# A GraphSAGE layer: destination one-hots in steps of 36 buckets, made apart from the source one-hots, and narrow tiles for the leftover one-hots

## Chip, cores, metric

The kernel runs on one core of a Trainium2 chip. The time is device microseconds of one launch. Comparisons are made between runs on the same chip; the profile is that of one further execution.

## What is computed

800,000 edges over 12,500 nodes with 64 features each. Each edge adds the features of its source node to its destination node; the sums are scaled by `deg_inv` and go through one 64 x 64 matrix, each node's own features through another.

```python
def reference(x, src, dst, deg_inv, w_self, w_neigh):
    N = x.shape[0]
    nsum = _segment_sum(x[src], dst, N)
    h_neigh = nsum * deg_inv[:, None]
    return x @ w_self + h_neigh @ w_neigh
```

`src` and `dst` are random, so nothing is known of the order of the edges.

## The kernel before

**Sorting.** Up to about 800 us the edges are sorted: each is a key made of its destination block (2 x 82 nodes, 77 blocks), its source block (128 nodes, 98 blocks) and the places in both. Edges with the same two blocks form a *bucket*; there are 77 x 98 = 7546 buckets (`NBID`), ordered by destination block. A bucket is held as 128 slots, 64 for each half (82 nodes) of its destination block. VectorE does the sorting and merging (L260, L316, L328). The buckets come in three parts, of 29, 20 and 10 buckets a row (`KPRS`), starting at buckets 0, 3712 and 6272 (`BASE`). Only the first part is ready when the last stage begins; the other two are merged and decoded beside it.

**Decoding.** `decode_buckets` (L766) writes the source places of a part to a DRAM tensor `sl` (one row of 128 slots a bucket) and turns its destination places by TensorE, so that each bucket becomes one column of an SBUF tile `dlT`. This tile has `TURN` columns; bucket b lies in column b modulo `TURN`, so the last part takes the place of the first. Before, `TURN` is 6272, the first multiple of 28 from `BASE[2]` on, and `SPARE`, the distance between the two, is 0. `turn` (L799) copies up to four buckets of each row at a time; for the last part, rows that lie before the wrap or across it get copies of their own (L815), the others one wide copy (L808).

**The last stage**, `nodes` (L943), runs in tiles of 8 buckets, some 950 tiles, each with these steps:

- `one_hots` (L924) makes, for 28 buckets at once, the source one-hots `ohs` (L935, one VectorE operation on the slots of `sl`, spread over all partitions by four DMAs of SP's queue into `slb`, L933) and right behind it the destination one-hots `ohd` (L940, one VectorE operation that compares columns of `dlT` with 0 to 81). `slb` and `ohs` have three buffers, `ohd` four.
- `gather` (L956) multiplies each bucket's source one-hot with the features of its source block on TensorE (L966), which fetches the source features of 128 edges into PSUM (`ct`, three buffers). ScalarE copies eight buckets of it to SBUF (`xg`, L976). After the last part is decoded (`self.changed`), VectorE takes some of these copies (L974): every other of those tiles at which the next tile will need new source one-hots.
- `sums` (L1027), two to five tiles later, multiplies the fetched features with the destination one-hots (L1047), 64 slots for each half, and adds them up in PSUM over six destination blocks (`OCT`). Then the matrix, the degree and the output follow (`finish`).

One-hots are made ahead: `gather` calls for more when fewer than `cnt + AHEAD` buckets are ready (8 + 44, and 8 + 36 once `self.changed`).

**Leftovers.** Edges that do not fit into their bucket's slots are collected apart. `pick` (L989) gathers their features by an indirect DMA of GpSimd's queue (L997), `spread` (L1002) makes their destination one-hots `ohl` (L1006) for only those destination blocks of the octet that the group can touch, from block f up to block e, and `add` (L1011) multiplies them into the same sums (L1015). The tile `ohl` has room for all six blocks of the octet in both halves, with five buffers (`HELD`).

**Order.** All of this stands under a schedule written by hand: each engine's instructions run in the order in which the program issues them. Between two tiles the program also issues merging operations on VectorE (L316, L328), as many as a pace allows (`PACE`, less what other VectorE work was put down in `self.spent`); the one-hots are not part of that count.

Of the kernel before, what the change touches and what calls it, by code (L numbers as in the profile page):

```python
# [14 lines left out]
FH = mybir.dt.float16  # L15
I32 = mybir.dt.int32
U32 = mybir.dt.uint32
OP = mybir.AluOpType
# [7 lines left out]
HN = 82  # L26
NDB = -(-N // (2 * HN))
NBID = NDB * NB
# [5 lines left out]
NP = len(KPRS)  # L34
ROWS = (128,) * NP
BASE = [128 * sum(KPRS[:p]) for p in range(NP)]
TURN = -(-BASE[2] // 28) * 28
SPARE = TURN - BASE[2]
assert 128 * KPRS[2] < BASE[1]
NCOL = 128 * sum(KPRS)  # L40
# [30 lines left out]
BEHIND = 5e3  # L71
NEARLY = 24
LAG = 4
HELD = 5
OCT = 6
OCTM = 256 // OCT + 1
# [297 lines left out]
class Kernel:  # L374
# [371 lines left out]
    def find_and_gather(self, part, vp):  # L746
# [7 lines left out]
        junk = vp.tile([128, max(n for _, n in WIN.w2[part])], BF, name="junk")  # L754
        for k in range(kpr + LAG):
            if k == 1:
                self.store_rows(part, nc.gpsimd)
            if k < kpr:
                self.count_below(part, k, acc, junk)
            if k >= LAG:  # L760
                g = k - LAG
                nc.scalar.activation(ix[:, g:g + 1], acc[:, g:g + 1], AF.Relu, bias=self.c2[part][:, 3, g:g + 1])
# [158 lines left out]
        self.left[part] = (place, s)  # L921
        yield 1

    def one_hots(self, pool):  # L924


        nc = self.nc
        for c in range(0, NBID, 28):
            n = min(28, NBID - c)
            b = pool.tile([128, 28 * 128], BF, name="slb", bufs=3)[:, :n * 128]  # L930
            src = self.sl[c:c + n]
            for j in range(4):
                nc.sync.dma_start(b[j::4], bass.AP(tensor=src.tensor, offset=src.offset, ap=[[0, 32], [1, n * 128]]))  # L933
            s = pool.tile([128, 28, 128], FH, name="ohs", bufs=3)[:, :n]
            nc.vector.tensor_scalar(s.rearrange("p c s -> p (c s)"), b, self.pidx[:, :1], None, op0=OP.is_equal)  # L935
            d = pool.tile([128, 14, HN, 2], FH, name="ohd", bufs=4)[:, :n // 2]
            at = c % TURN
            wide = [128, n // 2, HN, 2]
            ix = self.dlT[:, at:at + n].rearrange("p (c t) -> p c t", t=2)[:, :, None, :].to_broadcast(wide)
            nc.vector.tensor_tensor(d, self.iota[:, None].to_broadcast(wide), ix, op=OP.is_equal)  # L940
            yield [(s[:, j], d[:, j // 2, :, j % 2]) for j in range(n)]

    def nodes(self, pool, aps, mps):  # L943


        nc = self.nc
        source = self.one_hots(pool)
        ready = []
        pend = []
        late = []  # L950
        done = []
        acc = None
# [3 lines left out]
        def gather(b0, cnt, vector):  # L956

            nonlocal turn
            ct = aps.tile([128, 1024], F32, name="ct", bufs=3)
            ahead = AHEAD - 8 * vector  # L960
            while len(ready) < min(cnt + ahead, NBID - b0):
                ready.extend(next(source))
            cols = ready[:cnt]
            del ready[:cnt]
            for i in reversed(range(cnt)):
                nc.tensor.matmul(ct[:, i * 128:(i + 1) * 128], cols[i][0],  # L966
                                 self.xh[:, (b0 + i) % NB].rearrange("p a f -> p (a f)"), start=True, stop=True)
            xg = pool.tile([128, 1024], FH, name="xg", bufs=6)
            if vector and (len(ready) < min(8 + ahead, NBID - b0 - cnt) or NBID - b0 < 56):
                turn += 1  # L970
            else:
                vector = False
            if vector and turn % 2:
                nc.vector.tensor_copy(xg[:, :cnt * 128], ct[:, :cnt * 128])  # L974
            else:
                nc.scalar.activation(xg[:, :cnt * 128], ct[:, :cnt * 128], AF.Copy)  # L976
            return b0, xg, [d for _, d in cols]

        uses = []
        for o in range(-(-NDB // OCT)):  # L980
            lo, hi = o * OCT * NB, min((o + 1) * OCT * NB, NBID)
            for p in range(NP):
                for c in range(CHK[p]):
                    f = max(BASE[p] + c * GRP[p] * KPRS[p], lo)
                    e = min(BASE[p] + min((c + 1) * GRP[p], 128) * KPRS[p], hi)
# [3 lines left out]
        def pick(b0):  # L989
            if self.picked == len(done) or len([u for u in uses if u[5]]) >= HELD:  # L990
                return
            u = next((u for u in uses if not u[5]), None)
            if u and u[1] in self.left and b0 + LEAD >= u[4] * NB:
                _, p, c = u[:3]
                x = u[5] = pool.tile([128, 128], FH, name="lx", bufs=HELD)
                u[6] = len(done)
                nc.gpsimd.indirect_dma_start(  # L997
                    out=x, out_offset=None, in_=self.xt,
                    in_offset=bass.IndirectOffsetOnAxis(ap=self.left[p][1][:, c:c + 1].bitcast(U32), axis=0))
                self.picked = len(done)  # L1000

        def spread(u):  # L1002
            o, p, c, f, e = u[:5]
            u[7] = pool.tile([128, 2, OCT * HN], FH, name="ohl", bufs=HELD)
            n = slice((f - o * OCT) * HN, (e - o * OCT) * HN)
            nc.vector.tensor_scalar(u[7][:, :, n], self.wide.rearrange("p (h n) -> p h n", h=2)[:, :, n],  # L1006
                                    self.left[p][0][:, c:c + 1], -float(o * (OCT * HN + 4096)),
                                    op0=OP.subtract, op1=OP.is_equal)
            self.spent += 300

        def add(u, stop=False):  # L1011
            o, _, _, f, e = u[:5]
            n = slice((f - o * OCT) * HN, (e - o * OCT) * HN)
            for h in range(2):
                nc.tensor.matmul(acc[h][:, n], u[5], u[7][:, h, n], start=False, stop=stop)  # L1015

        def extras(b0, cnt):
            o = b0 // (OCT * NB)
            for u in uses[:HELD]:
                if u[5] and not u[7] and len(done) >= u[6] + 10 and b0 + 80 >= (u[4] - 1) * NB:  # L1020
                    spread(u)
                    break
            if uses and uses[0][7] and uses[0][0] == o and b0 + cnt > (uses[0][4] - 1) * NB and (
                    len(uses) > 1 and uses[1][0] == o):
                add(uses.pop(0))

        def sums(job):  # L1027
# [10 lines left out]
            if b0 + 24 >= end:  # L1038
                for u in uses:
                    if u[0] == o and not u[7]:  # L1040
                        assert u[5] and len(done) >= u[6] + 4
                        spread(u)
# [25 lines left out]
        for t, (b0, cnt) in enumerate(tiles):  # L1068
            pend.append(gather(b0, cnt, self.changed))
            if (len(pend) > 5) if self.changed else t % 2:  # L1070
                while len(pend) > (3 if self.changed else 2):
                    b0 = pend[0][0]
# [5 lines left out]
            b0 = tiles[t][0]  # L1078
# [130 lines left out]
    def after_sort(self, es, mps, aps):  # L1209
# [7 lines left out]
        with tc.manual_schedule():  # L1217
# [28 lines left out]
            for _ in self.merge_runs(LENA[0], u0, w0, NSUP):  # L1246
                if rows and not self.hold and next(rows, None) is None:
# [3 lines left out]
                    dl = es.enter_context(tc.tile_pool(name="dl", bufs=1, side="right"))  # L1251
                    self.dlT = dl.tile([128, TURN], BF, name="dlT")
            assert not rows
# [159 lines left out]
```

## Time and profile before

| | us |
|---|---|
| median of 3 runs | 1865.99 |
| lowest, highest | 1864.18, 1870.74 |
| the profiled execution | 1856.37 |
| its span, first to last instruction | 1854.6 |

In the profile, PE is TensorE's matmuls and PEld its weight loads, DVE is VectorE, ACT ScalarE, POOL GpSimd, SP the engine that issues most loads. A row of a group has the line, the engine, the operation, output and inputs, the shapes and the count, then busy time and the mean length in ns, then the idle time ahead of it and what ended it. A row of a wait names who waited for whom, with the total in us, how often, and the longest. A row of a stretch has the busy time and count of each engine, the granted TensorE clock as a share, the share of the DMA engines and GB/s.

### The profile page before, as it was taken

How to read it: one execution, taken by the hardware profiler on the slowest of the kernel's cores; microseconds unless marked ns; L12 is line 12 of the kernel's file. 1: busy time of each engine (PE TensorE's matmuls, PEld its weight loads, DVE VectorE, ACT ScalarE, POOL GpSimd, SP SyncE). 2: the span in 40 equal slices, each digit the busy share in tenths (PEclk: the TensorE clock that was granted, in tenths of full speed). 3: DMA queues.
4: the chain of work that ended last, by engine and by line, in shares of the span. 5: the costliest groups of instructions: out<-in, count | busy, mean ns of one | idle time of the engine just before them, and what ended most of it. 6: DMA issues, size and time to landing. Idle time of an engine off the chain costs nothing.

```text
span 1854.6 us, 54153 instructions
## 1 busy us (share of the span) xinstructions
PE 986.6 (53%) x23413; PEld 851.9 (46%) x23413; DVE 1718.2 (93%) x1718; ACT 1116.7 (60%) x1587; POOL 576.2 (31%) x447
## 2 busy tenths in 40 slices
PE   3046000000000000058979979897898899888996
PEld 1015000000000000057868868776887788777885
DVE  6999999999999999989989999998898799978885
ACT  5263000113001005458979989899999899977885
POOL 2000000055502005404456535473332523532331
PEclk7567555555555555579989999999999999999998
DMA  5207100021002002169978888996889788977894
GB/s 174 54 0 169 39 0 0 38 79 51 18 4 73 10 0 82 47 216 266 274 249 253 251 248 254 296 282 227 264 250 284 234 265 242 326 200 257 274 268 118
DMA packets 176789, 307.79 MB, mean 166 GB/s; under 512 B 127885, under 2 KB 133596, under 8 KB 175772
## 3 DMA queue, kind: packets, MB, share of 16 engines
q1 hardware_dynamic: 98268, 275.58, 44.9%
q0 software_dynamic: 78272, 28.65, 9.6%
q8 instruction: 185, 3.03, 0.7%
q14 instruction: 64, 0.52, 0.1%
HBM read 277.01 MB, written 26.52 MB: 164 GB/s over the span
## 4 chain that ended last, share of the span: by engine, by line
DVE 19%; PE 13%; DMA 11%; issue 10%; SPq 5%; POOL 4%; ACT 4%; DVEq 0%; POOLq 0%; ACTq 0%
DMA slb<-sl 10%; PE ct L966 7%; DVE u L328 7%; PE acc L1047 5%; SPq L933 5%; DVE ohs L935 4%; DVE ohd L940 3%; ACT xg L976 2%; DVE u L362 2%; POOL u L565 1%; POOL lx L997 1%; POOL out L1123 1%; DVE u L316 1%; DMA sl<-l 1%; PE acc L1015 1%
## 5 line engine op out<-in xcount | busy, mean ns | idle before, releaser
L976 ACT ACTIVATE xg<-ct 128x1024 f16<-128x1024 f32 x919 | 862.6, 1074 | 104.4 <-PE ct L966 80.0
L966 PE MATMUL ct<-xh,ohs 128*128 128x128 f16 x7546 | 532.6, 224 | 87.9 <-DVE ohs L935 23.7
L966 PEld LDWEIGHTS <-ohs 128*128 128x128 f16 x7546 | 451.8, 100 | 125.4 <-issue 52.5
L328 DVE TENSOR_TENSOR u<-u 128x1512 f32<-128x1512 f32 (+57 forms) x316 | 425.7, 1362 | 12.9 <-ACT u L312 8.6
L1047 PE MATMUL acc<-ohd,xg 64*128 64x82 f16 x15092 | 395.2, 201 | 47.7 <-ACT xg L976 20.4
L1047 PEld LDWEIGHTS <-xg 64*128 64x128 f16 x15092 | 324.6, 96 | 104.6 <-issue 29.2
L997 POOL DMA_INDIRECT lx<-xt,ls x127 | 232.0, 1826 | 425.6 <-PE acc L1015 352.5
L940 DVE TENSOR_TENSOR ohd<-iota,dlT 128x2296 f16<-128x2296 bf16 x270 | 362.2, 1341 | 0.0
L935 DVE TENSOR_SCALAR ohs<-slb,pidx 128x3584 f16<-128x3584 bf16 x270 | 321.8, 1192 | 40.2 <-DMA slb<-sl 19.0
L509 PE MATMUL stp<-cx,swapa 128*128 128x16 f32 (+1 forms) x12 | 3.1, 335 | 398.0 <-DVE swapa L505 398.0
L260 DVE TENSOR_TENSOR a<-b 128x1040 f32<-128x1040 f32 (+41 forms) x130 | 194.7, 1539 | 3.5 <-DVE b L260 0.5
L260 DVE TENSOR_TENSOR b<-a 128x1040 f32<-128x1040 f32 (+46 forms) x150 | 194.6, 1345 | 3.2 <-ACT a L262 0.4
L538 POOL DMA_INDIRECT u<-d,ixa x48 | 72.5, 1511 | 390.8 <-ACT junka L526 335.4
L509 PEld LDWEIGHTS stp<-cx,swapa 128*128 128x128 f32 x12 | 2.6, 271 | 398.5 <-DVE swapa L505 398.5
L312 ACT ACTIVATE u<-u 128x256 f32<-128x256 f32 (+14 forms) x60 | 33.0, 618 | 170.6 <-DVE u L316 134.8
L1123 POOL DMA_DIRECT2D out<-o x27 | 99.1, 3800 | 103.1 <-ACT o L1117 89.8
L802 PE MATMUL tr<-idb,l 128*128 128x128 bf16 x59 | 7.6, 263 | 188.9 <-ACT l L796 188.9
L262 ACT ACTIVATE b<-a 128x2 f32<-128x2 f32 (+31 forms) x41 | 15.9, 402 | 127.1 <-DVE a L260 120.4
L802 PEld LDWEIGHTS <-l 128*128 128x128 bf16 x59 | 4.3, 114 | 191.2 <-ACT l L796 190.8
L316 DVE TENSOR_TENSOR u<-u 128x2016 f32<-128x2016 f32 (+11 forms) x40 | 61.9, 1563 | 16.2 <-DMA u<-da,ixb 8.8
L262 ACT ACTIVATE a<-b 128x1 f32<-128x1 f32 (+24 forms) x34 | 8.6, 259 | 105.4 <-DVE b L260 99.9
L565 POOL DMA_INDIRECT u<-da,ixb x24 | 36.9, 1539 | 88.6 <-ACT ixb L513 85.0
(158 smaller groups left out, 839.4 us busy)
## 6 DMA issues: line engine op xcount, KB each, us to landing
slb<-sl SPq DMA_DIRECT2D x1076, 224.0 KB
xt<-xh SPq DMA_DIRECT2D x1, 3136.0 KB
out<-o POOLq DMA_DIRECT2D x25, 123.0 KB
own<-os SPq DMA_DIRECT2D x12, 256.0 KB
out<-os SPq DMA_DIRECT2D x12, 256.0 KB
rd<-dst SPq DMA_DIRECT2D x5, 512.0 KB
rs<-src SPq DMA_DIRECT2D x5, 512.0 KB
lx<-xt,ls POOLq DMA_INDIRECT x127
```

The costliest lines, as they stand in the source:

```text
L260: nc.vector.tensor_tensor(view(dst, lo + sh, [[st, g], [1, l]]), x, y, op=op)
L316: nc.vector.tensor_tensor(at(oth, to, n), x, y, op=op)
L328: nc.vector.tensor_tensor(to, at(cur, ln + lo, n), at(cur, lo + k, n), op=op)
L538: nc.gpsimd.indirect_dma_start(out=u[:, i * w:(i + 1) * w], out_offset=None, in_=src, in_offset=bass.IndirectOffsetOnAxis(ap=self.start[pa ...
L933: nc.sync.dma_start(b[j::4], bass.AP(tensor=src.tensor, offset=src.offset, ap=[[0, 32], [1, n * 128]]))
L935: nc.vector.tensor_scalar(s.rearrange("p c s -> p (c s)"), b, self.pidx[:, :1], None, op0=OP.is_equal)
L940: nc.vector.tensor_tensor(d, self.iota[:, None].to_broadcast(wide), ix, op=OP.is_equal)
L966: nc.tensor.matmul(ct[:, i * 128:(i + 1) * 128], cols[i][0], self.xh[:, (b0 + i) % NB].rearrange("p a f -> p (a f)"), start=True, stop=True)
L976: nc.scalar.activation(xg[:, :cnt * 128], ct[:, :cnt * 128], AF.Copy)
L997: nc.gpsimd.indirect_dma_start(out=x, out_offset=None, in_=self.xt, in_offset=bass.IndirectOffsetOnAxis(ap=self.left[p][1][:, c:c + 1].bit ...
L1047: nc.tensor.matmul(acc[h][:, db % OCT * HN:(db % OCT + 1) * HN], xg[r, i * 128:(i + 1) * 128], d[r], start=db % OCT == 0 and sb == 0, stop ...
L1123: nc.gpsimd.dma_start(out, o[:n, at], accum_op=OP.add)
```

## The change

Three things. The constant 28 in `TURN` becomes 36, which makes `TURN` 6300 and `SPARE` 28. `one_hots` falls into two generators: `source_hots` keeps its steps of 28, `dest_hots` makes destination one-hots in steps of 36 (`DCH`). `gather` draws from both, from whichever has fewer buckets ready, until both have enough. And the tile `ohl` becomes two blocks wide, filled from its start.

```diff
-TURN = -(-BASE[2] // 28) * 28
+TURN = -(-BASE[2] // 36) * 36
...
+DCH = 36
...
-    def one_hots(self, pool):
+    def source_hots(self, pool):
...
-            s = pool.tile([128, 28, 128], FH, name="ohs", bufs=3)[:, :n]
-            nc.vector.tensor_scalar(s.rearrange("p c s -> p (c s)"), b, self.pidx[:, :1], None, op0=OP.is_equal)
-            d = pool.tile([128, 14, HN, 2], FH, name="ohd", bufs=4)[:, :n // 2]
+            s = pool.tile([128, 28 * 128], FH, name="ohs", bufs=3)[:, :n * 128]
+            nc.vector.tensor_scalar(s, b, self.pidx[:, :1], None, op0=OP.is_equal)
+            yield [s[:, j * 128:(j + 1) * 128] for j in range(n)]
+
+    def dest_hots(self, pool):
+        nc = self.nc
+        for c in range(0, NBID, DCH):
+            n = min(DCH, NBID - c)
+            d = pool.tile([128, DCH // 2, HN, 2], FH, name="ohd", bufs=4)[:, :n // 2]
             at = c % TURN
             wide = [128, n // 2, HN, 2]
             ix = self.dlT[:, at:at + n].rearrange("p (c t) -> p c t", t=2)[:, :, None, :].to_broadcast(wide)
             nc.vector.tensor_tensor(d, self.iota[:, None].to_broadcast(wide), ix, op=OP.is_equal)
-            yield [(s[:, j], d[:, j // 2, :, j % 2]) for j in range(n)]
+            yield [d[:, j // 2, :, j % 2] for j in range(n)]
...
-        source = self.one_hots(pool)
-        ready = []
+        sources, dests = self.source_hots(pool), self.dest_hots(pool)
+        ready, spare = [], []
...
-            while len(ready) < min(cnt + ahead, NBID - b0):
-                ready.extend(next(source))
-            cols = ready[:cnt]
+            need = min(cnt + ahead, NBID - b0)
+            while min(len(ready), len(spare)) < need:
+                if len(ready) <= len(spare):
+                    ready.extend(next(sources))
+                else:
+                    spare.extend(next(dests))
+            cols = list(zip(ready[:cnt], spare[:cnt]))
             del ready[:cnt]
+            del spare[:cnt]
...
-            u[7] = pool.tile([128, 2, OCT * HN], FH, name="ohl", bufs=HELD)
+            assert e - f <= 2
+            u[7] = pool.tile([128, 2, 2 * HN], FH, name="ohl", bufs=HELD)
             n = slice((f - o * OCT) * HN, (e - o * OCT) * HN)
-            nc.vector.tensor_scalar(u[7][:, :, n], self.wide.rearrange("p (h n) -> p h n", h=2)[:, :, n],
+            nc.vector.tensor_scalar(u[7][:, :, :(e - f) * HN], self.wide.rearrange("p (h n) -> p h n", h=2)[:, :, n],
...
-                nc.tensor.matmul(acc[h][:, n], u[5], u[7][:, h, n], start=False, stop=stop)
+                nc.tensor.matmul(acc[h][:, n], u[5], u[7][:, h, :(e - f) * HN], start=False, stop=stop)
```

## The prediction

> **What bounds the kernel now.** I read the page's busy line and its slices first, then the stretches of the last stage, then what VectorE waits for there.
>
> ```profile
> span 1854.6 us, 54153 instructions
> PE 986.6 (53%) x23413; PEld 851.9 (46%) x23413; DVE 1718.2 (93%) x1718; ACT 1116.7 (60%) x1587; POOL 576.2 (31%) x447
> ...
> PE   3046000000000000058979979897898899888996
> ...
> DVE  6999999999999999989989999998898799978885
> ACT  5263000113001005458979989899999899977885
> ```
>
> TensorE has no work before about the seventeenth slice (some 800 us) except at the very start: until there VectorE sorts, alone. The changed lines run only from there on. So the table that counts is that of the last stage, cut where `nodes` starts to give VectorE some of the PSUM copies.
>
> ```profile
> core 0: us, PE busy (x) PEld busy (x) DVE busy (x) ACT busy (x) POOL busy (x), PEclk, DMA share, GB/s
> 800.00:1640.00 840.00, 734.61 (x18474) 648.69 (x18476) 783.15 (x936) 771.45 (x997) 366.67 (x212) 0.96 0.86 261
> 1640.00:1840.00 200.00, 176.00 (x4667) 158.87 (x4660) 173.99 (x210) 157.35 (x185) 51.25 (x26) 0.97 0.80 244
> ```
>
> Up to 1640 us VectorE is busy for 93% of the time, ScalarE for 92%, TensorE for 87%, and the DMA engines for 86%: four resources stand within a few per cent of each other, VectorE first. After 1640 us VectorE and TensorE stand at 87 to 88%. Finer stretches of 40 us show where VectorE alone is the bound:
>
> ```profile
> 880.00:920.00 40.00, 36.49 (x897) 32.36 (x890) 38.54 (x39) 39.86 (x66) 21.22 (x11) 0.94 0.90 268
> ...
> 1040.00:1080.00 40.00, 36.21 (x942) 32.24 (x942) 40.00 (x36) 37.96 (x50) 25.04 (x8) 1.00 0.81 236
> ...
> 1240.00:1280.00 40.00, 28.83 (x706) 24.23 (x705) 32.50 (x44) 38.00 (x56) 17.52 (x13) 1.00 0.79 251
> ...
> 1560.00:1600.00 40.00, 35.98 (x958) 31.21 (x955) 39.04 (x51) 38.57 (x52) 19.44 (x14) 1.00 0.92 298
> 1600.00:1640.00 40.00, 33.80 (x826) 29.77 (x822) 33.15 (x49) 38.89 (x60) 20.91 (x17) 0.96 0.80 253
> ```
>
> Of the 26 stretches from 800 to 1840 us, 13 have VectorE busy for 38.5 us or more (the first is 880 to 920, the last 1560 to 1600). There a nanosecond less on VectorE is a nanosecond less of time. In the other 13 it waits:
>
> ```profile
> DVE xg L974 <- PE ct L966: 19.4, 14, 3.2
> DVE ohs L935 <- DMA slb<-sl: 19.0, 15, 6.2
> DVE ohs L935 <- PE ct L966: 18.9, 18, 2.9
> DVE u L316 <- DMA u<-da,ixb: 7.3, 1, 7.3
> DVE u L316 <- DMA lx<-xt,ls: 7.0, 1, 7.0
> ```
>
> Each row has the total, the number of waits and the longest. Some are TensorE being late, some loads being late; no row says that a destination one-hot (`ohd`, L940) waits for its buffer.
>
> **What the change does to the work.** Destination one-hots: 7546 buckets were 269 operations of 28 and one of 14, 270 in all; in steps of 36 they are 209 and one of 22, 210 in all. The elements stay the same, so only what an instruction costs beside its elements goes, 60 times.
>
> ```profile
> L940 DVE TENSOR_TENSOR ohd<-iota,dlT 128x2296 f16<-128x2296 bf16 x269 | 361.4, 1344 | 0.0
> L935 DVE TENSOR_SCALAR ohs<-slb,pidx 128x3584 f16<-128x3584 bf16 x269 | 321.2, 1194 | 40.2 <-DMA slb<-sl 19.0 <-PE ct L966 18.9 <-PE acc L1047 1.0
> ```
>
> The rows above have the count, then busy time and mean ns of one, then idle time ahead; the next has the shortest, median and longest of all 270.
>
> ```profile
> L940 DVE TENSOR_TENSOR ohd<-iota,dlT x270: 751/1344/1403, 804.5 to 1832.6; 128x2296 f16<-128x2296 bf16 x135
> ```
>
> The odd one of 14 buckets has half the elements (14 x 82 = 1148) and is the minimum, 751 ns. So an element costs (1344 - 751) / 1148 = 0.517 ns, and the fixed part of a row is 1344 - 2296 x 0.517 = 158 ns. Rows of neighbours overlap, though:
>
> ```profile
> 1155.76 1.35 DVE L940 TENSOR_TENSOR ohd<-iota,dlT 128x2296 f16<-128x2296 bf16 x1
> 1157.03 0.26 DVE L1006 TENSOR_SCALAR ohl<-wide,lp 128x164 f16<-128x164 f16 x1
> 1157.96 1.68 DVE L935 TENSOR_SCALAR ohs<-slb,pidx 128x3584 f16<-128x3584 bf16 x1 [0.68 <-DMA slb<-sl]
> 1159.56 1.33 DVE L940 TENSOR_TENSOR ohd<-iota,dlT 128x2296 f16<-128x2296 bf16 x1
> 1160.82 2.90 DVE L328 TENSOR_TENSOR u<-u 128x1205 f32<-128x1205 f32 x2
> ```
>
> The first number is the start, the second the length. The instruction behind an `ohd` starts 1.26 to 1.27 us after it, while its row is 1.34 us long: some 79 ns lie under the next one. VectorE therefore pays 1.265 - 2296 x 0.517 / 1000 = 0.079 us of fixed cost for each. An operation of 36 buckets (2952 elements) should have a row of 1344 + 656 x 0.517 = 1683 ns and take 1.604 us to the next start. **Saved on VectorE: 60 x 0.079 = 4.7 us** (ends: 0 if 36 buckets cost more an element than 28, and 60 x 0.158 = 9.5 us if the whole fixed part counts).
>
> How much reaches the end: half of the stretches have VectorE full, which gives 2.35 us of the 4.7 in full. In the other half something else is late about as often as VectorE; I take half, 1.2 us. Together **3.5 us**; if all is on the path 4.7, if the other limits close up at once 0.
>
> Moved: in `nodes` a source operation is made when fewer than `cnt + AHEAD` columns are ready, a destination one when fewer than that are spare. Each stream alone follows the old rule, so every L935 and each of its four loads (L933, SP's queue) is issued at the same tile as before; only the L940s move. They no longer stand right behind an L935 but at tiles of their own, up to 44 buckets ahead of the matmul that gathers and more ahead of L1047 that reads them. No wait is added: four buffers of 36 hold 144 buckets instead of 112, and the 0.0 in the L940 row says that even 112 kept nothing waiting. So the larger buffers gain nothing either, and I cost them at 0.
>
> Leftover one-hots: the operation was already cut to its one or two blocks, only the tile was wide.
>
> ```profile
> L1006 DVE TENSOR_SCALAR ohl<-wide,lp 128x164 f16<-128x164 f16 x67 | 21.2, 320 | 0.0
> L1006 DVE TENSOR_SCALAR ohl<-wide,lp 128x328 f16<-128x328 f16 x60 | 19.0, 318 | 0.0
> ```
>
> 164 and 328 are 2 halves of 82 and of 164 columns, so the instructions stay as they are: 0 us. What it gives is room (5 x 2 x 2 x (492 - 164) = 6560 bytes a partition), which the wider `ohd` takes (4 x 8 x 82 x 2 = 5248).
>
> `TURN` becomes 6300, a multiple of 36, so 28 buckets of the last part lie before the wrap. In `turn` that takes three rows out of the wide copy and makes 9 small copies (L815) of 3, with their rows here:
>
> ```profile
> L815 ACT ACTIVATE dlT<-tr x3: 188/190/205, 1612.6 to 1625.0; 128x4 bf16<-128x4 bf16 x2, 128x2 bf16<-128x2 bf16 x1
> L805 ACT ACTIVATE dlT<-tr x13: 607/776/807, 740.9 to 1280.7; 128x512 bf16<-128x512 bf16 x12, 128x128 bf16<-128x128 bf16 x1
> ```
>
> Six more of 0.19 us are 1.1 us of ScalarE around 1612 to 1625 us, where it is the bound (38.89 of 40 in the row above); behind them wait the `xg` copies. Between 0 and 1.1 I take 0.5. Operations that straddle two parts now begin at buckets 3708 and 6264. The first is due at tile (3708 - 44) / 8 = 458, the second at 777.
>
> ```profile
> core 0: us, PE busy (x) PEld busy (x) DVE busy (x) ACT busy (x), PEclk, DMA share, GB/s
> 800.00:1280.00 480.00, 180.04 (x6712) 145.69 (x6712) 0.00 (x0) 397.79 (x424) 0.95 0.87 263
> 1280.00:1640.00 360.00, 141.48 (x5316) 115.29 (x5318) 2.12 (x2) 312.84 (x336) 0.96 0.84 259
> ```
>
> These are the copies `xg`, one a tile: 424 by 1280 us, about 760 by 1640, at 1.07 us a tile in the second stretch. So those tiles run near 1316 and 1658 us, over 30 us after the last writes of `dlT` that they need (1281 and 1625 us): no new wait.
>
> **Sum.** 3.5 - 0.5 = 3.0 us less. The profiled execution took 1856.37 us (span 1854.6), so **1853.4 us** for it. The median of the runs shown is 1865.99 us, 1.0052 times as much; on that scale the forecast is **1863.0 us**, 0.16% less.
>
> **Rivals.**
>
> *The whole row counts.* The fixed 158 ns would be paid in full, 9.5 us less, 1846.9 us (1856.4 on the median's scale). For it: VectorE has stretches of 40.00 in 40. Against it: the overlapping starts above. [...]
>
> *Moved operations fill waits.* L935 waits 33 times for slb or TensorE, 37.9 us without the L940 behind it being able to start. With the streams apart, an L940 can stand ahead of a waiting L935 and use the gap. A tile is 8 of 36 buckets, so about a quarter of the waits have one directly ahead: 0.25 x (37.9 - 6.2 for the first load) = 8 us, with the 3.0 above 11 us less, 1845.4 us (1855.0). Against it: where VectorE waits it is not the bound, and the filled time is soon lost to the engine that was late.
>
> *Slower: an L940 ahead of a PSUM copy on VectorE.* After 1640 us every other tile at which the ready columns are low gives its copy to VectorE.
>
> ```profile
> L974 DVE CAST xg<-ct 128x1024 f16<-128x1024 f32 x30 | 36.5, 1221 | 17.4 <-PE ct L966 16.2 <-ACT xg L976 1.1
> ```
>
> These tiles were chosen so that the pair of one-hots comes just after the copy. An L940 with a rhythm of its own falls on such a tile in 8 of 36 cases, and the copy starts up to 1.6 us later: 30 x 8 / 36 x 1.6 = 10.7 us if TensorE, with three `ct` buffers, stops for all of it (now its matmuls wait little for those copies:
>
> ```profile
> PE ct L966 <- DVE xg L974: 4.1, 4, 1.5
> ```
>
> in these 200 us). Less the 3.0 that is 7.7 us more, 1864.1 us (1873.7). It decides only if the delay exceeds the 0.58 us that a copy waits for its matmuls on average anyway (17.4 / 30), and if ScalarE has no slack to catch up; it has 21% there, which speaks against.
>
> *It doesn't pay.* Operations of 36 cost as much for a bucket as those of 28, or TensorE and the loads close up: 0, 1856.4 us (1866.0). DMA at 0.86 and ScalarE at 92% speak for it.
>
> **How the numbers follow.** A measurement here can tell about 0.3% (5.6 us) from no change. Chances: forecast 0.48 (own range 1860 to 1866), no pay 0.17, filled waits 0.13, whole row 0.10, slower 0.12. Both fast rivals lie beyond 0.3%, and 0.04 of the forecast's tail: faster 0.27. Slower 0.12. Same 0.61. The range takes in both fast rivals at the low end (1855.0, less 1 for the bounds of their terms) and at the high end no pay with all small copies and part of the slower case, 1871: 1854 to 1871, which leaves out some 0.15.
>
> **What would show it.** L940 should count 210 with rows near 1683 ns and a sum near 353 us; the start behind it 1.60 us later. If the rows are longer than 1.75 us, the saving is gone. VectorE's busy sum between 800 us and the end should fall by about 9 us in rows (of which half is overlap), its waits stay near their present sums. If the waits of L935 fall by several us, the waits were filled; if those of TensorE on L974 (4.1 us now) rise by several, the slower rival holds. L815 should count 9. L935 and L933 should keep 270 and 1080 rows. The time before 797 us should not move: a difference there would be none of this change's, and would make the prediction wrong for a reason not treated here.

## The result, and the profile after

| | runs | median us | lowest, highest |
|---|---|---|---|
| before | 7 | 1866.93 | 1863.31, 1870.74 |
| after | 7 | 1875.92 | 1868.78, 1880.45 |

The ratio is 1.0051, with a 95% interval of 1.0032 to 1.0070: **slower by half a per cent, 9 us**, where 0.16% less was forecast, and beyond the range. The profiled execution of the changed kernel took 1868.78 us (span 1867.1), 12.4 us more than that of the kernel before. Of the runs further below, three that took over 1.5% longer than the fastest of their kernel are left out of every comparison: two of the kernel before (2115 and 2778 us) and one of `e_early` (1892 us).

The page of the changed kernel gives the span, the busy sums (engine, us, share of the span, instructions) and, of its groups, the ones that the change touches. Behind the change the lines are shifted: L936 makes the source one-hots, L949 the destination ones, L980 fetches, L990 and L988 copy, L1062 adds up, L1011 gathers the leftovers.

```profile
span 1867.1 us, 54098 instructions
...
PE 1005.2 (54%) x23413; PEld 861.5 (46%) x23413; DVE 1716.4 (92%) x1658; ACT 1117.5 (60%) x1593; POOL 606.8 (33%) x447
...
L1011 POOL DMA_INDIRECT lx<-xt,ls x127 | 268.9, 2117 | 423.9 <-PE acc L1030 346.8
...
L936 DVE TENSOR_SCALAR ohs<-slb,pidx 128x3584 f16<-128x3584 bf16 x270 | 321.1, 1191 | 56.6 <-DMA slb<-sl 21.3
L949 DVE TENSOR_TENSOR ohd<-iota,dlT 128x2952 f16<-128x2952 bf16 x210 | 353.6, 1684 | 0.0
```

VectorE has the 60 instructions less that were counted, 1658 for 1718, but its busy time fell by 1.8 us alone. Two other things moved. GpSimd (POOL) is busy 30.6 us longer with the same 447 instructions, and its leftover gather takes 2117 ns on the mean where it took 1826, as the row of the kernel before has it:

```profile
L997 POOL DMA_INDIRECT lx<-xt,ls x127 | 232.0, 1826 | 425.6 <-PE acc L1015 352.5
```

And source one-hots wait 56.6 us, where they waited 40.2; 10.4 of them are one wait at 1449 to 1459 us.

Where is the time lost? The count of fetch matmuls in a stretch (`ct`, 28 for each source one-hot) is a clock of progress. Here are the stretches for that one line, first of the kernel before, then of the changed one; the columns are TensorE's matmuls and weight loads, the granted clock, the DMA engines' share, GB/s.

```profile
800.00:1240.00 440.00, 224.59 (x3149) 189.28 (x3150) 0.95 0.88 264
1240.00:1300.00 60.00, 27.81 (x392) 23.61 (x393) 0.97 0.75 242
```

```profile
800.00:1240.00 440.00, 224.92 (x3148) 188.99 (x3148) 0.95 0.87 264
1240.00:1300.00 60.00, 26.27 (x354) 22.28 (x355) 0.94 0.70 215
```

Up to 1240 us the two kernels are level, 3149 and 3148 matmuls after 440 us. In the next 60 us the changed one does 38 fewer; at 60 us for 392 that is 5.8 us. The rest of the 12.4 us is lost in later stretches. At 1240 to 1300 us part 1 is decoded beside the last stage, and the waits there (who waited for whom: total us, times, longest) name the place. Changed kernel, 1240 to 1290 us:

```profile
PE acc L1062 <- ACT xg L990: 10.3, 4, 5.8
DVE w L783 <- ACT l L793: 6.6, 1, 6.6
...
ACT l L797 <- DMA sl<-l: 4.3, 1, 4.3
```

And the kernel before, the same stretch:

```profile
PE acc L1047 <- ACT xg L976: 8.0, 5, 2.4
...
DVE w L782 <- ACT l L792: 3.8, 2, 2.3
...
ACT l L791 <- DMA sl<-l: 1.0, 1, 1.0
```

Read from the bottom up. ScalarE waits for the store of source slots to `sl`, 4.3 us and not 1.0; TensorE then waits up to 5.8 us for ScalarE's copies `xg`, and VectorE 6.6 us for ScalarE. ScalarE's timeline in the changed kernel (start, length, operation, idle time ahead in brackets) shows that wait between the two copies of the second group of slots. In parts 1 and 2 `l16` has two buffers, and one still belongs to the store of the first group.

```profile
1253.51 0.63 ACT L793 ACTIVATE l<-w 128x512 bf16<-128x512 int32 x1
...
1259.53 0.63 ACT L793 ACTIVATE l<-w 128x512 bf16<-128x512 int32 x1
1264.51 0.63 ACT L797 ACTIVATE l<-v 128x512 bf16<-128x512 int32 x1 [4.35 <-DMA sl<-l]
1265.05 2.83 ACT L990 ACTIVATE xg<-ct 128x1024 f16<-128x1024 f32 x3
```

The first group was copied by 1254.14 (1253.51 + 0.63). Its store is issued by GpSimd, whose timeline follows, changed kernel first:

```profile
1235.34 1.58 POOL L743 DMA_INDIRECT v<-d,ix  x1 [0.30 <-ACT xg L990]
1237.22 4.05 POOL L1011 DMA_INDIRECT lx<-xt,ls  x1 [0.30 <-issue]
1241.58 3.21 POOL L1011 DMA_INDIRECT lx<-xt,ls  x1 [0.30 <-PE ct L980]
1245.09 1.44 POOL L743 DMA_INDIRECT v<-d,ix  x1 [0.30 <-ACT xg L990]
...
1255.60 1.24 POOL L1011 DMA_INDIRECT lx<-xt,ls  x1 [0.30 <-issue]
1256.78 0.66 POOL L795 DMA_DIRECT2D sl<-l  x1
```

```profile
1234.75 0.95 POOL L997 DMA_INDIRECT lx<-xt,ls  x1 [0.30 <-issue]
1236.01 1.58 POOL L997 DMA_INDIRECT lx<-xt,ls  x1 [0.30 <-issue]
...
1249.78 1.70 POOL L997 DMA_INDIRECT lx<-xt,ls  x1 [0.30 <-issue]
1252.60 0.58 POOL L794 DMA_DIRECT2D sl<-l  x1 [1.12 <-ACT l L792]
```

Before, GpSimd was idle for 1.12 us and issued the store 0.3 us behind the copy. Now it comes straight from other work, 2.6 us late (1256.78 - 1254.14). In this time its queue holds the same instructions in the same order, yet it reached the first leftover gather 2.5 us later than before (1237.22 for 1234.75), was through with the second 7.2 us later (1244.79 for 1237.59), and made up some of that in the gathers behind. These two gathers, 0.95 and 1.58 us long before, took 4.05 and 3.21. What kept them? VectorE's timeline of the changed kernel, over the same time:

```profile
1235.66 1.15 DVE L936 TENSOR_SCALAR ohs<-slb,pidx 128x3584 f16<-128x3584 bf16 x1
1236.72 0.94 DVE L329 TENSOR_TENSOR u<-u 128x756 f32<-128x756 f32 x1
1237.57 1.69 DVE L949 TENSOR_TENSOR ohd<-iota,dlT 128x2952 f16<-128x2952 bf16 x1
1239.18 0.91 DVE L329 TENSOR_TENSOR u<-u 128x728 f32<-128x728 f32 x1
1240.01 1.15 DVE L936 TENSOR_SCALAR ohs<-slb,pidx 128x3584 f16<-128x3584 bf16 x1
1241.07 0.93 DVE L329 TENSOR_TENSOR u<-u 128x744 f32<-128x744 f32 x1
1241.91 1.69 DVE L949 TENSOR_TENSOR ohd<-iota,dlT 128x2952 f16<-128x2952 bf16 x1
1243.52 1.15 DVE L936 TENSOR_SCALAR ohs<-slb,pidx 128x3584 f16<-128x3584 bf16 x1
```

The first gather ends at 1241.27, the second source one-hot L936 at 1241.16; the second gather ends at 1244.79, the third L936 at 1244.67. Both end 0.11 to 0.12 us after a source one-hot has ended. Each held GpSimd from just behind one source one-hot to the end of the next. Three operations lie between the first two L936 here, two between the next. Over the 75 source one-hots from 960 to 1240 us, the distance from start to start has a standard deviation of 0.97 us in the changed kernel and 0.67 in the one before. That this unevenness is what stretches the gathers is not shown, and `e_half28` below speaks against it.

This is no chance of two rows. In 16 profiles of this case, 522 of GpSimd's gather issues after 800 us took over 2.4 us. Of them 440 ended between 0.05 and 0.20 us after the end of a source one-hot (25 of 29 in the kernel before, 38 of 44 in the changed one), and none that close behind a destination one-hot. Of 932 issues of at most 1.3 us 98 did. Those during which VectorE was idle (187) took 0.95 us in the median. In the rows above one issue stood for 4.05 us beside four operations and ended only behind the source one-hot; which of the four held it, they do not tell, and by what means is not shown.

One thing adds to the loss. The stretches of 1260 to 1274 us in the changed kernel (busy time and count of each engine, granted clock, DMA share, GB/s):

```profile
1260.00:1262.00 2.00, 0.35 (x16) 0.20 (x12) 1.94 (x5) 0.16 (x1) 1.24 (x2) 1.00 1.08 370
1262.00:1264.00 2.00, 0.00 (x0) 0.00 (x0) 2.00 (x3) 0.00 (x0) 0.60 (x1) 1.00 0.97 336
1264.00:1266.00 2.00, 0.00 (x0) 0.00 (x0) 0.26 (x1) 1.49 (x3) 0.00 (x0) 0.77 0.92 283
1266.00:1268.00 2.00, 1.89 (x29) 1.77 (x30) 0.00 (x0) 2.00 (x4) 0.64 (x1) 0.50 0.73 266
1268.00:1270.00 2.00, 2.00 (x38) 1.80 (x37) 0.00 (x0) 1.97 (x4) 0.34 (x1) 0.50 0.17 31
1270.00:1272.00 2.00, 2.00 (x30) 1.85 (x24) 1.14 (x3) 1.97 (x5) 0.58 (x1) 0.52 0.05 8
1272.00:1274.00 2.00, 1.79 (x47) 1.43 (x45) 1.86 (x3) 2.00 (x4) 0.00 (x0) 1.00 0.18 66
```

TensorE stands still for 5.8 us, from 1260.35 to 1266.11, and when it goes on the granted clock is 0.50 until about 1272 us.

The late issue is only half of the store's delay. The store lands in 16 parts, each counted in the trace. Before, the last part came 5.3 us after the issue (1257.89); now it comes after 7.6 us (1264.36), 1.9 us behind the fifteenth. So it lands 10.2 us behind ScalarE's copy and not 5.6, and of these 4.6 us the issue makes 2.3. The DMA engines are full in this time (1.08, 0.97), but so they were before (1.03, 0.92, 0.97 and 1.03 from 1252 to 1260 us), so that does not explain it. Over the profiles below in which GpSimd issues the store, it landed 4.0 to 5.8 us after an issue in time, and 6.8 to 13.9 us after one that GpSimd's own work had made late. Why the last part comes late is open.

### The profile page after: what moved, and what is told of

Its sections match the earlier page's. It is cut to its first block, busy times and chain, and to the rows that moved or that the text cites. A ratio compares the mean times of both kernels' runs of the same rounds, so it can differ in the third digit from the quotient of the medians.

```text
span 1867.1 us, 54098 instructions
## 1 busy us (share of the span) xinstructions
PE 1005.2 (54%) x23413; PEld 861.5 (46%) x23413; DVE 1716.4 (92%) x1658; ACT 1117.5 (60%) x1593; POOL 606.8 (33%) x447
## 4 chain that ended last, share of the span: by engine, by line
PE 16%; DVE 16%; DMA 10%; issue 9%; ACT 9%; SPq 5%; POOL 2%; DVEq 0%; another core or an unknown queue 0%; ACTq 0%; POOLq 0%
DMA slb<-sl 9%; PE ct L980 9%; PE acc L1062 6%; ACT xg L990 6%; DVE u L329 6%; SPq L934 5%; DVE ohs L936 3%; DVE ohd L949 2%; DVE u L363 2%; DVE u L317 1%; ACT u L313 1%; POOL u L566 1%; PE acc L1030 1%; PE po L1129 1%; DVE ohl L1021 1%
## 5 line engine op out<-in xcount | busy, mean ns | idle before, releaser
L990 ACT ACTIVATE xg<-ct 128x1024 f16<-128x1024 f32 x919 | 863.7, 1070 | 120.1 <-PE ct L980 72.0
L980 PE MATMUL ct<-xh,ohs 128*128 128x128 f16 x7546 | 535.0, 224 | 79.9 <-ACT xg L990 22.1
L980 PEld LDWEIGHTS <-ohs 128*128 128x128 f16 x7546 | 452.7, 100 | 117.5 <-issue 47.3
L1062 PE MATMUL acc<-ohd,xg 64*128 64x82 f16 x15092 | 405.3, 201 | 61.2 <-issue 30.5
L1011 POOL DMA_INDIRECT lx<-xt,ls x127 | 268.9, 2117 | 423.9 <-PE acc L1030 346.8
L1062 PEld LDWEIGHTS <-xg 64*128 64x128 f16 x15092 | 328.1, 96 | 125.1 <-issue 52.2
L936 DVE TENSOR_SCALAR ohs<-slb,pidx 128x3584 f16<-128x3584 bf16 x270 | 321.1, 1191 | 56.6 <-DMA slb<-sl 21.3
L949 DVE TENSOR_TENSOR ohd<-iota,dlT 128x2952 f16<-128x2952 bf16 x210 | 353.6, 1684 | 0.0
L566 POOL DMA_INDIRECT u<-da,ixb x24 | 34.1, 1419 | 89.3 <-ACT ixb L514 85.4
```

Of the source, the lines that this page charges most:

```text
L936: nc.vector.tensor_scalar(s, b, self.pidx[:, :1], None, op0=OP.is_equal)
L980: nc.tensor.matmul(ct[:, i * 128:(i + 1) * 128], cols[i][0], self.xh[:, (b0 + i) % NB].rearrange("p a f -> p (a f)"), start=True, stop=True)
L1011: nc.gpsimd.indirect_dma_start(out=x, out_offset=None, in_=self.xt, in_offset=bass.IndirectOffsetOnAxis(ap=self.left[p][1][:, c:c + 1].bit ...
L1062: nc.tensor.matmul(acc[h][:, db % OCT * HN:(db % OCT + 1) * HN], xg[r, i * 128:(i + 1) * 128], d[r], start=db % OCT == 0 and sb == 0, stop ...
```

## Experiments

**Theory A**, which grew out of the first runs: the loss is made where part 1 is decoded, by the chain above: uneven source one-hots, stretched gathers, a late store, ScalarE's wait for a buffer, TensorE behind it. Its links are tested one by one, and not all of them held. **Theory B**: the new rhythm costs a little in many places. Ratios are to the kernel before, run on the same chip between them; below 1 is faster.

To compare the profiles, the text gives two numbers of each: how late GpSimd issued the first store of part 1 after ScalarE's copy, and how long the nine source one-hots around the decode took (from the start of the 118th to that of the 127th). Before they are 0.3 and 41.7 us, after 2.6 and 46.4.

### The parts of the change

**Old lengths, old order, narrow `ohl`.**

```diff
-DCH = 36
+DCH = 28
```

> The changed kernel with destination steps of 28 again: the streams draw in step, so every L940 stands right behind its source one-hots as before, while TURN 6300, the small copies in turn and the narrow ohl tile stay. If the order or the length of the destination operations makes the loss: ratio 1.000 (0.998 to 1.002). If the rest of the change makes it (copies, addresses, room): 1.005.

Measured: 0.9986 (0.9964 to 1.0008). Late 0.3, nine one-hots 42.1 us. The narrow leftover tiles and the wrap at 6300 cost nothing.

**28 in an even rhythm of their own**: the first operation makes 14 buckets.

```diff
-TURN = -(-BASE[2] // 36) * 36
+TURN = 14 + -(-BASE[2] // 28) * 28
-DCH = 36
+DCH = 28
...
-        for c in range(0, NBID, DCH):
-            n = min(DCH, NBID - c)
+        for c in (0, *range(14, NBID, DCH)):
+            n = min(DCH if c else 14, NBID - c)
```

> Destination steps of 28, but the first one of 14, so that each destination operation comes half a step away from the source operations; 271 operations of the old length, evenly spaced (TURN 6286). If it is enough that the two stand apart: 1.005. If it is the uneven spacing that 36 against 28 makes, or the length of 36: 1.000.

Measured: 0.9989 (0.9968 to 1.0010). Late 0.3, 41.8 us. Two streams half a step apart are no loss when both have the same step. But the leftover gathers are stretched here too, 2098 ns on the mean, as in the changed kernel (2117), although the source one-hots come as evenly as before (standard deviation 0.69 us). So it does not take uneven source one-hots to stretch the gathers, and stretched gathers alone cost no time that shows.

**36, but only right behind a source one-hot**, so that nothing but the count of operations changes in the order.

```diff
-            while min(len(ready), len(spare)) < need:
-                if len(ready) <= len(spare):
-                    ready.extend(next(sources))
-                else:
+            while len(ready) < need:
+                ready.extend(next(sources))
+                goal = need + (len(ready) - need) // 8 * 8 if len(ready) >= need else len(ready)
+                while len(spare) < min(goal, NBID - b0):
                     spare.extend(next(dests))
```

> Destination steps of 36, each issued only right behind a source operation of the same tile (7 of 9 source operations have one behind them). If a destination operation ahead of a source operation makes the loss: the saving of 60 operations remains, 0.997 to 0.999. If long operations or uneven distances between source operations make it: 1.003 to 1.005.

Measured: 1.0004 (0.9981 to 1.0028). Late 0.3, 40.8 us. The 60 instructions less bring no gain that can be measured. The source one-hots are as uneven as in the changed kernel (1.04 us; gathers 2020 ns), and no loss shows.

**Twice as many destination operations**: the kernel before with each cut in two of half the length, 270 more.

```diff
-            nc.vector.tensor_tensor(d, self.iota[:, None].to_broadcast(wide), ix, op=OP.is_equal)
+            for a, e in ((0, n // 4), (n // 4, n // 2)):
+                nc.vector.tensor_tensor(d[:, a:e], self.iota[:, None].to_broadcast([128, e - a, HN, 2]), ix[:, a:e], op=OP.is_equal)
```

> The kernel before with each destination operation cut into two of 14 buckets, one right behind the other: 269 operations more of equal spacing. If VectorE pays 79 ns for each and three quarters of it reach the end, as the prediction had it: 16 us more, 1.0085. If the fixed part does not reach the end at all: 1.000. If the whole 158 ns counts: 1.017 to 1.022.

Measured: 1.0040 (1.0017 to 1.0063), 7 us. At 0.079 us each, 270 operations are 21 us of VectorE, so about a third reached the end (by the interval 3 to 12 us). And its profile shows the same stall, 3.1 us late and 47.4 us for the nine: some 5 of the 7 us may be that. So the fixed cost of an operation seems to count little here.

### Where the loss is made

**The changed kernel again.**

> The changed kernel again, unaltered, beside the others of this call. If its loss is its own and not the scatter of the first seven runs: 1.003 to 1.007. If the first runs were scatter: 0.998 to 1.002.

Measured: 1.0039 (1.0017 to 1.0060). Late 2.6, nine one-hots 46.7 us; the two gathers took 4.0 and 3.2 us again. The stall repeats.

**Apart only before about 1640 us, apart only after.** In the changed kernel one more loop ahead of the old one makes destination one-hots behind source ones in the other part; `e_early` asks `while vector and ...`, `e_late` `while not vector and ...`.

```diff
+            while vector and len(ready) < need:
+                ready.extend(next(sources))
+                goal = need + (len(ready) - need) // 8 * 8 if len(ready) >= need else len(ready)
+                while len(spare) < min(goal, NBID - b0):
+                    spare.extend(next(dests))
             while min(len(ready), len(spare)) < need:
```

> The opposite: a rhythm of their own until about 1640 us, behind the source operations after it. If destination operations ahead of source operations in the stage that VectorE bounds make the loss: 1.004 to 1.006. If the copies of the last 200 us make it: 1.000 to 1.001.

> Destination steps of 36, behind the source operations until VectorE takes copies (about 1640 us), and with a rhythm of their own after that, as in the changed kernel. If the loss comes from a destination operation ahead of a PSUM copy on VectorE in the last 200 us: 1.004 to 1.006. If it comes from the stage before: 1.000 to 1.001, as with all of them behind source operations (1.0004).

Measured: early 1.0032 (1.0009 to 1.0055), late 2.6, 45.2 us; late 1.0022 (0.9992 to 1.0052), late 2.2, 45.8 us. The first says that the loss does not need the tail, where VectorE shares the copies. The second is inconclusive: up to about 1650 us VectorE's operations in it are those of `e_behind36`, in the same order, and still its profile has the stall, which that of `e_behind36` has not. So the stall depends on small shifts in time, not on the order alone, and one profile does not say how often a kernel has it.

**Another phase**: a first operation of 18 buckets, the others of 36.

```diff
-TURN = -(-BASE[2] // 36) * 36
+TURN = 18 + -(-(BASE[2] - 18) // 36) * 36
...
-        for c in range(0, NBID, DCH):
-            n = min(DCH, NBID - c)
+        for c in (0, *range(18, NBID, DCH)):
+            n = min(DCH if c else 18, NBID - c)
```

> The changed kernel with a first destination step of 18, so that all later ones fall at other tiles (TURN 6282). If two rhythms of 28 and 36 cost time wherever they meet: 1.004 to 1.006, like the changed kernel. If the loss hangs on a few places where a destination operation happens to stand ahead of something that all wait for: anything from 0.998 to 1.003.

Measured: 0.9999 (0.9976 to 1.0022). Late 0.3, nine one-hots 39.5 us. Almost the same operations (211), nearly as uneven (0.89 us), half a step aside: the loss is gone, and no gain is there.

### Taking the wait away, and making it

**Four buffers of `l16`** in all parts, at both places where the tile is made; the same in the kernel before; and with the phase of 18.

```diff
-            l16 = vp.tile([128, 4, 128], BF, name="l16", bufs=2 if part else 4)
+            l16 = vp.tile([128, 4, 128], BF, name="l16", bufs=4)
```

> The changed kernel with four buffers of l16 in every part instead of two in parts 1 and 2, so that ScalarE's copy of the second group of destination slots no longer waits for the store of the first group's source slots. Theory A (the loss is made where part 1 is decoded: a late store of source slots, ScalarE's 4.35 us wait for it, and TensorE and VectorE behind ScalarE): the wait is gone although GpSimd still issues the store some 2.5 us late; the ratio to the kernel before falls from 1.004-1.005 to 0.999-1.001, 6 to 9 us less than the changed kernel. Theory B (the uneven rhythm of the source one-hots costs a little in many places): at most 2 us go, ratio 1.003-1.005.

> The control: the kernel before with four buffers of l16 in every part. There ScalarE waits only 1.03 us for the store. Theory A and theory B: ratio 0.999-1.000, at most 1 us less.

> The changed kernel with a first step of 18 buckets in the stream of destination one-hots, and four buffers of l16 in every part: the version hoped to beat both. Theory A: neither a late issue nor a wait for a buffer is left at the decode of part 1, and the saving on VectorE stays, ratio 0.996-0.999. Theory B: no better than the same kernel with two buffers, 0.9999, so 0.999-1.002.

Measured: after 0.9989 (0.9967 to 1.0012), before **0.9967 (0.9945 to 0.9989)**, phase 1.0000 (0.9976 to 1.0024). By the two ratios, four buffers take about half a per cent off the changed kernel. But its profiled run, one of its slower ones, still has a wait:

```profile
1262.03 0.63 ACT L793 ACTIVATE l<-w 128x512 bf16<-128x512 int32 x1
1267.80 0.63 ACT L797 ACTIVATE l<-v 128x512 bf16<-128x512 int32 x1 [5.13 <-DMA sl<-l]
```

It stands one group later, with a store 3.0 us late and 45.5 us for the nine one-hots. That store landed 13.9 us after its issue: 15 of its parts were there after 6.4 us, at 1260.07, and the last came at 1267.56. So four buffers do not rule the wait out. That the kernel before gains 0.3% from them was not expected: its own waits may be longer in other executions than the 1.0 us of the profiled one. With four buffers its twelve runs lie within 8.4 us; the 33 compared without them lie within 21 us. And the best phase gains nothing from them, as theory B had it.

**A late store, made in the kernel before.** Small memsets stand in GpSimd's queue ahead of that one store.

```diff
+PAUSES = 18
...
+            if part == 1 and k == 0:
+                self.pause(PAUSES)
             (nc.gpsimd if part else nc.sync).dma_start(rows[:, k:k + n], l16[:, :n])
```

> The kernel before with 18 memsets of about 0.2 us each put into GpSimd's queue ahead of the store of part 1's first group of source slots and nowhere else, so that this one store is issued some 2.5 us later with the old order and the old even rhythm. Theory A: ScalarE waits 3 to 4 us where it waited 1.0, and the kernel is slower, ratio 1.002-1.003 (3 to 6 us). Theory B: one pause of GpSimd costs nothing by itself, ratio 0.999-1.001.

Measured: 1.0021 (0.9998 to 1.0044). The pause came out longer than meant, 6.39 us, so the store was 5.9 us late. GpSimd, TensorE and ScalarE in it:

```profile
1248.70 6.39 POOL L426 MEMSET pad<- 128x100 f32 x18
1255.43 0.58 POOL L797 DMA_DIRECT2D sl<-l  x1 [0.34 <-issue]
```

```profile
1259.50 0.72 ACT L792 ACTIVATE l<-w,edge 128x512 bf16<-128x512 int32 x1 [5.35 <-DMA sl<-l]
```

```profile
1262.46 0.73 PE L1050 MATMUL acc<-ohd,xg 64*128 64x82 f16 x16 [6.75 <-ACT xg L979]
```

The whole second half of the chain stands there with the old order and nothing else changed: ScalarE waits 5.35 us, TensorE 6.75, the nine one-hots take 47.2 us. Its store was later than the changed kernel's, but landed 4.0 us after its issue. What it costs in the end is some 4 us, at the edge of what the interval tells from none.

**A tile of their own for the source slots**, so that destination slots never meet a store's buffer (three buffers in the changed kernel, two in the kernel before).

```diff
-            l16 = vp.tile([128, 4, 128], BF, name="l16", bufs=2 if part else 4)
+            l16 = vp.tile([128, 4, 128], BF, name="s16" if part else "l16", bufs=3 if part else 4)
```

> The changed kernel with a tile of their own, of three buffers, for the source slots of parts 1 and 2 (the destination slots keep two), so that no copy of destination slots can meet a buffer that a store still reads, and a copy of source slots only that of three groups, 18 us, before. Theory A (late store, ScalarE's wait for it, TensorE and VectorE behind ScalarE): no wait of ScalarE for a store at the decode of part 1, its stretch of 126-117 source one-hots takes 40 to 42 us and not 46, ratio 0.998-1.000, and within 0.1% of x_before_own. Theory B (the uneven rhythm costs elsewhere): the wait goes, and the kernel stays 0.2% or more above x_before_own.

> The control: the kernel before with a tile of their own, of two buffers, for the source slots of parts 1 and 2. Both theories: the old wait of about 1 us goes, ratio 0.996-0.999 as with four buffers of one tile (0.9967).

Measured: after 0.9999 (0.9974 to 1.0023), before 0.9975 (0.9953 to 0.9996). The profile of the changed one has its store 2.8 us late, as ever, and no wait for it; the nine one-hots take 41.7 us. So a late store without the wait costs nothing at that place. The profile of the kernel before has, by chance, the opposite. GpSimd's timeline:

```profile
1245.37 4.03 POOL L1123 DMA_DIRECT2D out<-o  x1
1249.71 1.94 POOL L742 DMA_INDIRECT v<-d,ix  x1 [0.30 <-ACT xg L976]
1251.94 1.28 POOL L997 DMA_INDIRECT lx<-xt,ls  x1 [0.30 <-PE acc L1015]
1253.22 1.64 POOL L794 DMA_DIRECT2D sl<-s  x2
```

And ScalarE, when it needs the buffer of that store again:

```profile
1265.55 0.72 ACT L791 ACTIVATE s<-w,edge 128x512 bf16<-128x512 int32 x1 [8.55 <-DMA sl<-s]
```

ScalarE had copied the first group by 1246.31, and GpSimd, busy with an output and two gathers, came 6.9 us late. The store then took 12.2 us to land, its last part 7.2 us behind the others on record. ScalarE waited 8.55 us, though the nine one-hots lost only 3.7 us (45.4). So the old order can have the stall too: it hangs on who comes first at GpSimd's queue and on when the last part of the store lands.

**The store issued by ScalarE itself.**

```diff
-            (nc.gpsimd if part else nc.sync).dma_start(rows[:, k:k + n], l16[:, :n])
+            (nc.scalar if part else nc.sync).dma_start(rows[:, k:k + n], l16[:, :n])
```

> The changed kernel with the stores of source slots of parts 1 and 2 issued by ScalarE itself, right behind its copy, and not through GpSimd's queue; two buffers as before. Theory A, whose first link is that GpSimd came to the store 2.6 us late: the store starts within 0.5 us of the copy, ScalarE's wait falls from 4.35 us to 1 or 2, ratio 0.999-1.001. If the wait stays at 4 us with a store in time, the link from GpSimd's queue to the wait is wrong (the transfer itself is slow there): ratio 1.003-1.005.

> The control: the kernel before with the same stores issued by ScalarE. GpSimd was in time there (0.3 us behind the copy), so nothing is gained and ScalarE pays for eight issues: ratio 0.999-1.002.

Measured: after 1.0026 (1.0004 to 1.0048), before 1.0023 (0.9996 to 1.0050). The store is in time, and ScalarE's wait in the changed kernel fell to 1.35 us. But the issue itself now stands in ScalarE's queue: the copy behind it starts some 0.56 us later, and one such copy waited 2.05 us, by the profile for a gather. The nine one-hots stay long in both kernels (45.7 and 44.7). Theory A's ratio of 0.999 to 1.001 did not come. It is no remedy, and does not settle the link from GpSimd's queue.

### What they say together

| pair | changed to unchanged (95%) |
|---|---|
| as given, 7 runs of each | 1.0051 (1.0032 to 1.0070) |
| as given, the repeat | 1.0039 (1.0017 to 1.0060) |
| four buffers in both | 1.0025 (1.0008 to 1.0043) |
| a tile of their own in both | 1.0024 (1.0003 to 1.0045) |
| store by ScalarE in both | 1.0007 (0.9984 to 1.0029) |
| four buffers in both, changed one with the phase of 18 | 1.0030 (1.0010 to 1.0050) |

The last four are worked out from the means of the twelve runs of each kernel and their spread. Theory A holds for its place from the late store on. Where GpSimd issued the store in time, the nine one-hots took 39.5 to 42.1 us; where it was late and ScalarE waited, 45.2 to 47.4; late without a wait they took 41.7 (its own tile) and 37.6 (the phase of 18 with four buffers, 1.9 us late). By the ratios that is about half of the loss, an estimate, since their intervals overlap. Theory A's beginning, that uneven source one-hots make the store late, is not shown.

With the wait taken out the changed kernel is still about a quarter of a per cent slower than the kernel before treated alike, and so is the phase of 18 with four buffers (0.3%). The profiles place a part of it. Around 1419 to 1462 us (from the start of the 161st source one-hot to that of the 171st) the eight kernels with steps of 28 or 14 took 42.0 to 44.6 us and the ten with steps of 36 took 45.3 to 48.1, whatever their phase and buffers: 2.9 us more on the mean. In this stretch VectorE has one long wait (1395 to 1480 us; first the kernel before, then the changed one):

```profile
DVE u L316 <- DMA lx<-xt,ls: 7.0, 1, 7.0
```

```profile
DVE ohs L936 <- remote: 10.4, 1, 10.4
```

**What makes it longer stays open.** GpSimd's gathers are stretched all through: what their issues after 800 us took beyond 0.95 us adds up to 138 us before and 172 after. But `e_half28` has 169 and the phase of 18 has 159, and neither is slower than the kernel before.

The version that beats both is the kernel before with four buffers of `l16`: 0.9967 (0.9945 to 0.9989).

## Why the prediction was wrong

**Right: the sizes of the moved operations.** 210 operations, a sum of 353.6 us and a mean of 1684 ns were forecast as 210, 353 and 1683; the next instruction starts 1.61 us behind one (1237.57 to 1239.18), forecast 1.60. L816 makes nine copies. Before 797 us nothing moved: VectorE is busy 760.89 us there before and 761.09 after. From there on its busy time fell by 2.0 us (957.33 to 955.35), less than the 4.7 worked out: the leftover one-hots, costed at 0, took 340 ns each where they had taken 319, 2.7 us in all.

**Too high: what reaches the end.** 3.5 of 4.7 us, three quarters, were put on the path. With the destination one-hots kept behind the source one-hots, 60 operations less showed no gain (1.0004), and 270 more cost about a third of theirs, stall included. The interval of the first, 0.9981 to 1.0028, leaves room for the 3.0 us that were forecast; it does not show them.

**The step that failed: "No wait is added", and ahead of it "only the L940s move".** The second is true of the order in which instructions are issued, and not of what goes on beside them. The working followed the moved operations on VectorE's queue, on SP's, and past their own buffers. It did not ask what else runs while they run. GpSimd's queue was left out of the sum, though its gathers grow longer beside the moved one-hots (2117 ns and not 1826 on the mean; what in the new order does it is not shown), and a store stands behind those gathers for which ScalarE waits. The wait that was added is none of a one-hot: it is ScalarE's for `sl`, 1.0 us before and 4.35 after, and some 5 us of the loss come with it. The row that could have warned was on the page before: the leftover gathers' mean of 1826 ns, twice the 0.95 us of the shortest. The other part of the loss is placed only in part, and its cause is open.

**The rivals.** The slower rival had the right sign and the wrong place; that its 1873.7 us lie near the measured 1875.92 is luck. It wanted TensorE to wait more for VectorE's copies after 1640 us; where it waited 4.1 us for them before, it now waits 1.6, and `e_early`, apart only before 1640 us, is about as slow as the change (1.0032). The rival that moved operations would fill waits of source one-hots fell the other way: these waits did not shrink, they rose from 40.2 to 56.6 us. That the whole row counts is refuted by the start 1.61 us behind a row of 1.69.

## What to carry to other kernels

When operations of VectorE are moved, look at what GpSimd issues beside them: if the issue times of one kind of DMA scatter several-fold (the leftover gathers of the kernel before: 0.94 to 5.03 us), ask what holds them; the store that stood behind them in that queue came 2.6 us late in the changed kernel. Where a store gives a buffer back to a busy engine, count the buffers by the latest landing (13.9 us after the issue here), not by the usual one (4 to 6). And a few microseconds saved on an engine that is busy for 93% of the time are easily lost to one late store (some 5 us here), when four resources stand that close together (86 to 93% up to 1640 us).

## What the hardware showed unexpectedly

After 800 us a gather's issue by GpSimd took 0.95 us in the median while VectorE was idle (0.94 to 0.98 us for the 22 of the kernels before and after) and up to 5.24 us beside it (before; 4.95 after), and a long one mostly ended 0.05 to 0.20 us behind one kind of VectorE operation, the source one-hots (440 of 522 over 2.4 us). In the timeline above it had not ended behind any of the three operations in between.

ScalarE's copy that waited for the store of one group of slots started at 1264.51 us, 0.15 us behind the last of its 16 parts (1264.36), and that part came far behind the others: 1.9 us behind the fifteenth in the changed kernel, 7.5 us in the profile with four buffers.

In 5.8 us without matmuls TensorE's granted clock fell to 0.50, and it stayed there from about 1265 to 1272 us, so this stall cost more than its length: 16 fetch matmuls took 1.91 us in that time (from 1267.31 us) and 1.05 ahead of the stall (from 1258.87 us). The matmuls ran for 5.8 us (1266.11 to 1271.9) before the clock was full.
